# Attention with beacon keys and a gated feed-forward: value products of batches 2 and 3 over 64-row halves

## The chip, the cores and the metric

The kernel runs on one core of one Trainium2 chip. The metric is the device time of one execution in microseconds, lower is better; the time before is the median of three runs. Engines are named as the profile names them: PE is TensorE's matrix products and PEld its weight loads, DVE is VectorE, ACT is ScalarE, POOL is GpSimd and SP is SyncE. The "q" behind an engine's name stands for its queue, in which it also issues transfers (DMAs).

## The reference

There are 8 batches, 8 heads, 576 tokens and a head size of 64. Each batch and head has 16 beacon keys and values, which every query sees; among the tokens themselves the mask is causal. The heads' outputs are put side by side as 512 columns for 4608 tokens and go through a gated feed-forward of width 1536.

```python
k_all = np.concatenate([beacon_k, k], axis=2)
v_all = np.concatenate([beacon_v, v], axis=2)
scores = scale * np.matmul(q, k_all.transpose(0, 1, 3, 2))
scores = np.where(causal, -1000000000.0, scores)
a = np.exp(scores - scores.max(-1, keepdims=True))
a /= a.sum(-1, keepdims=True) + 1e-09
attn = np.matmul(a, v_all)
...
g = x @ w_gate
out = (g * (1.0 / (1.0 + np.exp(-g))) * (x @ w_val)) @ w_out
```

## The kernel before

**Pairs.** Two heads make a pair, so a batch has 4 pairs and the whole has 32. Pair n belongs to batch n // 4: pairs 0 to 3 are batch 0, pairs 8 to 15 are batches 2 and 3. The 592 keys of a head lie in 5 blocks of 128, the last one half filled. The 576 queries lie in 5 blocks (`QBLOCKS`), and query block c needs the key blocks 0 to c, so a head has 1 + 2 + 3 + 4 + 5 = 15 value products (batch 0 does its first two query blocks elsewhere, in `pv_front`).

**What one pair goes through.** Scores for four units A to D (`scores`, TensorE, tile s_ps), the exponential (`exponent`, ScalarE, line 379, tile p), the mask on the diagonal (`mask`, VectorE line 388 or POOL line 392), then the value products (`pv`, TensorE, tile pv_ps), whose stationary side is a block of p, 128 keys by 128 queries, and whose moving side is 64 columns of values and a column of ones that gives the sum. `normalize` (VectorE: the reciprocal at line 493, the product at line 494) writes x. When a batch's four pairs are normalized, `x_transpose` (line 519) makes SP issue five transposes by DMA, x to xT; the gate and value products (`gate_value`, tile gv_ps) read xT, and `project` (tile o_ps) makes the output.

**Two ways of doing the value products.** The constant `WIDE` (line 34) chooses by batch. In batches below `WIDE` the first pass (letter P of the plan) does the 15 products of the pair's first head and the second pass (letter p) those of the second, each over all 128 rows of a key block: line 465. In the other batches every product is cut in two over 64 rows of the key block (rows 0 to 63 and 64 to 127), and each pass has 30 of them. The first pass takes rows 0 to 63 for head 0 and rows 64 to 127 for head 1, in turn; the second pass takes the other half for each. Each head has its own bank of pv_ps. These go through `halves`, whose product stands at line 151, as do all scores, gate, value and output products, which are cut into 64-row halves throughout. When a bank is about to be written from the other row half than before, `halves` first puts in an instruction that waits for the last product into that tile:

```python
if was is not None and was[0] != row:
    last = max((w for (i, _), w in writers.items() if i == at[0]), key=lambda w: w[2])
    if was[3]:
        after(nc.tensor.nop(), last[1], "one bank, two row halves")
```

**What sets the order.** One long string, the plan, written out by hand: each letter emits one piece of work, and every engine takes its instructions in that order. S or s are scores, E an exponential, D or M a mask on VectorE or POOL, P and p the two passes, R a normalization, G and H the two passes of a gate and value unit, F output products, O and o evacuations, V the five transposes x to xT, t one transpose of keys or queries by SP, and l one load issued by POOL. After the first 24, a load waits on POOL for a product two pieces back, so TensorE's progress paces the loads. Four PSUM tiles of two banks each (`take`, `give`) go round among scores, value products, gate units and output.

The letters around the passes of pairs 8 to 15 are

```
8:  Pp          9: PMDtMp      10: PEOlp      11: PEMp
12: PDlRp      13: PlEp        14: PEMDp      15: Pp
```

of which E, M, D, t, O, l and R put nothing on TensorE. After pair 9 pair 10 follows, and after pair 11 pair 12, also with nothing on TensorE between (`oD`, and none). Among the later pairs, over 64-row halves, pair 16 has `PlFFp`, pair 17 `PESFlp`, pair 19 `Pa2Ep` (a and 2 are not on TensorE), and pairs 22 and 23 together `P1Pp2p`.

Of the kernel before, what the change touches and what calls it, by code (L numbers as in the profile page):

```python
# [30 lines left out]
ROWS = S // HALF  # L31


WIDE = 4


FREE_LOADS = 24
# [33 lines left out]
def kernel(  # L71
# [381 lines left out]
    def pv(n, second):  # L453
# [4 lines left out]
        o_ps = pvs[n]  # L458
        if b < WIDE:

# [355 lines left out]
```

## Time and profile before

| | |
|---|---|
| median of 3 runs | 369.63 us (368.88 to 370.25) |
| the profiled execution | 369.36 us, span 367.6 us |
| granted TensorE clock, mean | 0.999 |
| value products over 128 rows (L465) | 456 in pairs 0 to 15, 18.5 to 143.6 us |
| value products over 64 rows (L151) | 960 in pairs 16 to 31, 144.0 to 281.5 us |

The span goes from the first to the last instruction of the profiled execution; the time is that of the whole execution and a little longer. In the profile's first part each engine has its busy time, its share of the span and its count of instructions. The chain that ended last is followed back from the last instruction, at each step to what released it. In a timeline each row is a start in microseconds, a length, the engine, the line, the operation with output and inputs, how many were merged, and in square brackets how long the engine had been idle and what the profile names as the reason. A wait for several semaphores is put down to one of them, which need not be the right one. The slices of the page, 40 equal parts of the span with busy tenths, tell where transfers fill the core's 16 DMA engines:

```profile
PE   7799999989999999999999999999999999999996
...
DMA  8999999999999999999598309301330201100113
```

TensorE's tenths stay at 9 from the tenth slice on; the DMA engines are nearly full up to about the twentieth slice, some 175 us, which takes in pairs 8 to 15.

### The profile page before, as it was taken

How to read it: one execution, taken by the hardware profiler on the slowest of the kernel's cores; microseconds unless marked ns; L12 is line 12 of the kernel's file. 1: busy time of each engine (PE TensorE's matmuls, PEld its weight loads, DVE VectorE, ACT ScalarE, POOL GpSimd, SP SyncE). 2: the span in 40 equal slices, each digit the busy share in tenths (PEclk: the TensorE clock that was granted, in tenths of full speed). 3: DMA queues.
4: the chain of work that ended last, by engine and by line, in shares of the span. 5: the costliest groups of instructions: out<-in, count | busy, mean ns of one | idle time of the engine just before them, and what ended most of it. 6: DMA issues, size and time to landing. Idle time of an engine off the chain costs nothing.

```text
span 367.6 us, 11647 instructions
## 1 busy us (share of the span) xinstructions
PE 355.6 (97%) x5037; PEld 219.9 (60%) x5037; DVE 227.1 (62%) x429; ACT 185.9 (51%) x276; POOL 124.6 (34%) x201
## 2 busy tenths in 40 slices
PE   7799999989999999999999999999999999999996
PEld 3588565655565555555665567556766555555554
DVE  4577786548764676277636683767568735766631
ACT  3874688953576651736774458237913322322201
POOL 8862456972366286770350027000200000000000
PEclk9999999999999999999999999999999999999999
DMA  8999999999999999999598309301330201100113
GB/s 147 162 193 201 204 164 160 147 170 176 158 127 176 175 115 107 112 201 150 63 180 101 86 7 124 67 0 59 68 116 14 54 13 46 60 3 0 60 59 114
DMA packets 143988, 39.88 MB, mean 108 GB/s; under 512 B 130368, under 2 KB 139328, under 8 KB 143936
## 3 DMA queue, kind: packets, MB, share of 16 engines
q0 software_dynamic: 95424, 18.85, 73.0%
q1 hardware_dynamic: 48224, 19.92, 30.1%
q8 instruction: 39, 0.64, 0.7%
q10 hardware_dynamic: 288, 0.36, 0.3%
q14 instruction: 13, 0.11, 0.1%
HBM read 38.27 MB, written 9.44 MB: 130 GB/s over the span
## 4 chain that ended last, share of the span: by engine, by line
PE 88%; DMA 4%; DVE 3%; ACT 2%; issue 1%; POOL 1%; SPq 1%; POOLq 0%; ACTq 0%
PE gv_ps L151 51%; PE o_ps L151 23%; PE s_ps L151 6%; PE pv_ps L151 4%; PE pv_ps L465 4%; DMA xT<-x 2%; DMA qk<-in_q_dram 2%; PE t_ps L283 1%; ACT p L379 1%; DVE x L494 1%; SPq L519 1%; DVE x L427 0%; DVE kT L246 0%; POOL qk L193 0%; DVE p L388 0%
## 5 line engine op out<-in xcount | busy, mean ns | idle before, releaser
L151 PE MATMUL gv_ps<-xT,wg 64*128 64x512 bf16 (+2 forms) x912 | 196.0, 365 | 2.2 <-DVE p L388 1.9
L151 PE MATMUL gv_ps<-xT,wv 64*128 64x512 bf16 (+2 forms) x912 | 197.2, 365 | 0.0
L379 ACT ACTIVATE p<-s_ps 128x832 bf16<-128x832 f32 (+2 forms) x127 | 104.2, 867 | 36.8 <-PE s_ps L151 35.3
L551 ACT ACTIVATE th<-gv_ps 128x512 f32<-128x512 f32 (+2 forms) x114 | 65.5, 574 | 112.1 <-PE gv_ps L151 111.2
L151 PE MATMUL o_ps<-wo,hT 64*128 64x512 bf16 (+2 forms) x912 | 113.9, 365 | 0.2
L556 DVE SCALAR_TENSOR_TENSOR u<-th,gv_ps 128x512 f32<-128x512 f32 (+2 forms) x114 | 74.9, 657 | 59.3 <-ACT th L551 59.0
L151 PEld LDWEIGHTS <-wg 64*128 64x128 bf16 x912 | 83.9, 94 | 41.4 <-issue 1.9
L151 PEld LDWEIGHTS <-wv 64*128 64x128 bf16 x912 | 83.6, 94 | 35.2 <-issue 0.5
L563 DVE SCALAR_TENSOR_TENSOR hT<-gv_ps,u 128x512 bf16<-128x512 f32 (+2 forms) x114 | 75.2, 663 | 3.6
L151 PEld LDWEIGHTS <-hT 64*128 64x128 bf16 x912 | 46.7, 94 | 30.0 <-PE o_ps L151 1.2
L392 POOL TENSOR_SCALAR_AFFINE_SELECT p<-p 128x256 bf16<-128x256 bf16 (+2 forms) x66 | 25.3, 405 | 74.6 <-ACT p L379 72.3
L151 PE MATMUL s_ps<-qT,kT 64*128 64x336 bf16 (+3 forms) x512 | 45.0, 250 | 2.2 <-DVE kT L246 0.5
L202 POOL DMA_DIRECT2D vb<-in_v_dram x40 | 34.0, 854 | 22.7 <-PE gv_ps L151 15.9
L151 PEld LDWEIGHTS <-kT 64*128 64x128 bf16 x512 | 25.2, 94 | 21.9 <-DVE kT L246 1.2
L388 DVE TENSOR_TENSOR p<-p,upper 128x256 bf16<-128x256 bf16 (+2 forms) x77 | 21.4, 298 | 22.3 <-ACT p L379 21.2
L494 DVE TENSOR_TENSOR x<-pv_ps,rec 128x640 bf16<-128x640 f32 (+1 forms) x32 | 25.3, 791 | 1.2
L202 POOL DMA_DIRECT2D qk<-in_q_dram x25 | 21.3, 852 | 11.0 <-PE pv_ps L465 3.5
L246 DVE COPY o_sb<-o_ps 128x512 f32<-128x512 f32 (+2 forms) x22 | 14.0, 663 | 17.8 <-PE o_ps L151 12.8
L202 POOL DMA_DIRECT2D qk<-in_k_dram x25 | 21.1, 844 | 9.3 <-PE s_ps L151 3.9
L493 DVE RECIPROCAL rec<-pv_ps 128x10 f32<-128x10 f32 (+1 forms) x32 | 6.9, 215 | 24.2 <-PE pv_ps L151 16.2
L151 PEld LDWEIGHTS <-p 64*128 64x128 bf16 x960 | 18.4, 94 | 3.4 <-DVE x L494 0.2
L244 ACT ACTIVATE o_sb<-o_ps 128x512 f32<-128x512 f32 (+2 forms) x16 | 8.7, 570 | 22.5 <-PE o_ps L151 21.7
(63 smaller groups left out, 136.6 us busy)
## 6 DMA issues: line engine op xcount, KB each, us to landing
out_dram<-o_sb SPq DMA_DIRECT2D x34, 256.0 KB, 3.4
vb<-in_v_dram POOLq DMA_DIRECT2D x24, 128.0 KB, 7.1
qk<-in_q_dram POOLq DMA_DIRECT2D x20, 128.0 KB, 6.4
qk<-in_k_dram POOLq DMA_DIRECT2D x15, 128.0 KB, 6.8
wv<-in_moe_w_val_dram POOLq DMA_DIRECT2D x4, 384.0 KB, 8.9
wg<-in_moe_w_gate_dram POOLq DMA_DIRECT2D x4, 384.0 KB, 8.7
wo<-in_moe_w_out_dram POOLq DMA_DIRECT2D x2, 768.0 KB, 15.1
qk<-in_k_dram POOLq DMA_DIRECT2D x2, 576.0 KB, 13.4
```

Source lines behind the costliest of these rows:

```text
L151: ins = nc.tensor.matmul(o, lhsT=l, rhs=r, start=start, stop=stop)
L202: return nc.gpsimd.dma_start(dst[p0 : p0 + n, c, :, 0:D], src[b, :, r : r + n, :].rearrange("h j d -> j h d"))
L244: nc.scalar.activation(o, i, ACT.Copy)
L246: eng.tensor_copy(o, i)
L379: nc.scalar.activation(p_of(b, m, u == "A")[:, :, c0 : c0 + w], ps[:, :, 0:w], ACT.Exp, scale=0.125)
L388: nc.vector.tensor_tensor(out=ap, in0=ap, in1=upper[:, None, d : d + w].to_broadcast([P, 2, w]), op=ALU.mult)
L392: nc.gpsimd.affine_select(out=ap, in_=ap, compare_op=ALU.is_ge, fill=0.0, base=d, pattern=[[0, 2], [1, w]], channel_multiplier=-1,)
L465: ins = nc.tensor.matmul(o_ps[:, side, 68 * c : 68 * c + D + 1], lhsT=pt[n % NPT][:, side, col : col + P], rhs=vb[b % 2][:, t, 2 * m + sid ...
L494: nc.vector.tensor_tensor(out=xs[b][:, c0:NKT, P * m : P * m + P].rearrange("p c (h d) -> p h c d", d=D), in0=o[:, :, :, 0:D], in1=rec[:, ...
L551: nc.scalar.activation(th[:, 0:w], gvs[n][:, 0, 0:w], ACT.Tanh, scale=0.5)
L556: nc.vector.scalar_tensor_tensor(out=u[:, 0:w], in0=ths[n][:, 0:w], scalar=1.0, in1=gvs[n][:, 0, 0:w], op0=ALU.add, op1=ALU.mult)
L563: nc.vector.scalar_tensor_tensor(out=hTs[j][:, f, c0:c1], in0=gvs.pop(n)[:, 1, 0 : c1 - c0], scalar=0.5, in1=ths.pop(n)[:, 0 : c1 - c0], o ...
```

## The change

One constant goes from 4 to 2, so that `pv` takes the path over 64-row halves from batch 2 on:

```diff
-WIDE = 4
+WIDE = 2
```

The two paths in `pv`, the first of which batches 2 and 3 leave and the second of which they take:

```python
        if b < WIDE:
            ...
                    ins = nc.tensor.matmul(
                        o_ps[:, side, 68 * c : 68 * c + D + 1],
                        lhsT=pt[n % NPT][:, side, col : col + P],
                        rhs=vb[b % 2][:, t, 2 * m + side, 0 : D + 1],
            ...
                for row in (1, 0) if second else (0, 1):
                    hh = row ^ second
                    r = slice(HALF * row, HALF * row + HALF)
                    halves(
                        ("p", n), hh, row, o_ps[:, hh, 68 * c : 68 * c + D + 1],
                        pt[n % NPT][r, hh, col : col + P], vb[b % 2][r, t, 2 * m + hh, 0 : D + 1],
```

In pairs 8 to 15 a pass thus has 30 weight loads and 30 products over 64 rows, of 128 and 65 columns, where it had 15 and 15 over 128 rows; and `halves` puts its wait between the two passes of each pair. Batches 0 and 1 keep whole rows, batches 4 to 7 keep halves. The plan, the loads and the work of the other engines are as before.

## The prediction

> **What bounds the kernel now.** I read the page first: its opening lines and the chain that ended last.
>
> ```profile
> span 367.6 us, 11647 instructions
> PE 355.6 (97%) x5037; PEld 219.9 (60%) x5037; DVE 227.1 (62%) x429; ACT 185.9 (51%) x276; POOL 124.6 (34%) x201
> PE 88%; DMA 4%; DVE 3%; ACT 2%; issue 1%; POOL 1%; SPq 1%; POOLq 0%; ACTq 0%
> ```
>
> TensorE is busy for 97% of the span and is 88% of the chain. So a microsecond more on TensorE is a microsecond more at the end, unless TensorE would have waited there anyway. Two questions follow: what the eight changed head pairs cost on TensorE, and where TensorE waits behind them. The view of the tile pv_ps has the two forms side by side (nanoseconds min/median/max, first and last start):
>
> ```profile
> L151 PE MATMUL pv_ps<-vb,p x960: 187/189/201, 144.0 to 281.5; 64*128 64x65 bf16 x192
> L465 PE MATMUL pv_ps<-vb,p x456: 190/193/205, 18.5 to 143.6; 128*128 128x65 bf16 x152
> ```
>
> The 189 and 193 ns are latencies of overlapping products and say nothing of the pace. The pace is read from starts, in TensorE's timeline (start, length, operation, count). Pair 13 alone, and pairs 11 and 12 together, over 128 rows:
>
> ```profile
> 110.61 0.34 PE L151 MATMUL s_ps<-qT,kT 64*128 64x240 bf16 x4
> 110.88 1.08 PE L465 MATMUL pv_ps<-vb,p 128*128 128x65 bf16 x30
> 111.90 0.35 PE L151 MATMUL s_ps<-qT,kT 64*128 64x336 bf16 x4
> ```
> ```profile
> 103.38 0.40 PE L151 MATMUL o_ps<-wo,hT 64*128 64x512 bf16 x2
> 103.71 1.99 PE L465 MATMUL pv_ps<-vb,p 128*128 128x65 bf16 x60
> 105.63 0.37 PE L151 MATMUL s_ps<-qT,kT 64*128 64x336 bf16 x4
> ```
>
> The two passes of pair 17, over 64-row halves, apart from each other:
>
> ```profile
> 150.09 0.32 PE L151 MATMUL s_ps<-qT,kT 64*128 64x240 bf16 x4
> 150.25 0.61 PE L151 MATMUL pv_ps<-vb,p 64*128 64x65 bf16 x30
> 150.70 0.34 PE L151 MATMUL s_ps<-qT,kT 64*128 64x336 bf16 x4
> 150.88 0.38 PE L151 MATMUL o_ps<-wo,hT 64*128 64x512 bf16 x2
> 151.09 0.61 PE L151 MATMUL pv_ps<-vb,p 64*128 64x65 bf16 x30
> ```
>
> And pair 19, the one pair over halves whose second pass follows its first with nothing between on TensorE (two windows, the second opening after the first pass ends):
>
> ```profile
> 177.52 0.36 PE L151 MATMUL s_ps<-qT,kT 64*128 64x336 bf16 x4
> 177.70 0.64 PE L151 MATMUL pv_ps<-vb,p 64*128 64x65 bf16 x30
> ```
> ```profile
> 178.40 0.23 PE L151 MATMUL pv_ps<-vb,p 64*128 64x65 bf16 x4
> ```
>
> **The change, part by part.** The built program shows it on TensorE alone: each pair 8 to 15 gets 60 loads and 60 products over 64 rows for 30 and 30 over 128, 240 products more in all; every other queue keeps its order.
>
> *Products.* A pass of 30 half products takes 150.70 - 150.25 = 0.45 us, so two half products, one on each row half, start within 30 ns. A pair over 128 rows takes 111.90 - 110.88 = 1.02, or 34 ns a product with what lies at its edges. Doubling the count therefore costs nothing in pace: 2 x 0.45 = 0.90 against 1.02.
>
> The Trainium skill has a rule that speaks against the change ("TensorE: Matmul & The Clock Gate", section "LDWEIGHTS (loading the stationary operand)"): a weight load takes time by its columns, not by its rows, about 128/1.2 = 107 ns, so a 64-row load is no cheaper than a 128-row one. If loads were served one after another, an estimate from that page is 30 x 107 ns = 3.2 us more for each pair and 26 us in all. The rows of pair 17 deny this: two loads and two products pass in 30 ns, so loads for the two row halves overlap, and I put nothing for them.
>
> *Edges.* From the 240-column scores to the first wide product is 110.88 - 110.61 = 0.27 us; to the first half product it is 150.25 - 150.09 = 0.16. TensorE pays about 0.1 where it passes from half rows to whole rows. The way out is similar: the last wide product of pair 13 starts at 111.77 and the next score at 111.90, 0.13 later, against 0.03 at pair 17. Both go away.
>
> *The new wait.* The second pass writes each bank from the other row half, and `halves` puts a wait on the first pass's last product before it. At pair 19 the second pass starts 178.40 - 177.70 = 0.70 after the first, where a pass takes 0.45: the wait costs 0.25. In all of pairs 8 to 15 the written order has nothing on TensorE between the passes, so all eight pay it. Behind the waiting load stands all of TensorE's queue; ScalarE's exponentials wait for the scores in it, and VectorE's reciprocals for the pair's last product.
>
> *Sum.* A single pair between scores: before 111.90 - 110.61 = 1.29; after 0.16 + 0.70 + 0.45 = 1.31, so +0.02. Bounds 0.00 to +0.05: a pass read at 0.44 to 0.455, before other neighbours. A double, pairs 11 and 12: before 105.63 - 103.38 = 2.25; after 0.21 (151.09 - 150.88) + 2 x (0.70 + 0.45) = 2.51, so +0.26: the edges are saved once, the wait is paid twice. Pairs 9 and 10 between scores: 77.51 - 75.30 = 2.21 before, 0.18 + 2.30 = 2.48 after, +0.27. Pairs 8, 13, 14 and 15 are singles. In all 4 x 0.02 + 0.26 + 0.27 = **+0.61 us** on TensorE (0.5 to 0.75).
>
> **What TensorE waits for behind them.** TensorE's waits from 66 to 146 us, then two rows of its timeline and one of the transfers issued at 70.59:
>
> ```profile
> PE gv_ps L151 <- DVE p L388: 1.9, 2, 1.4
> ```
> ```profile
> 79.24 0.37 PE L151 MATMUL gv_ps<-xT,wg 64*128 64x512 bf16 x1 [1.38 <-DVE p L388]
> ```
> ```profile
> 155.44 0.37 PE L151 MATMUL gv_ps<-xT,wg 64*128 64x512 bf16 x1 [0.19 <-DMA xT<-x]
> ```
> ```profile
> xT<-x SPq DMA_TRANSPOSE x1, 8.5
> ```
>
> The name VectorE in two of them misleads. This gate product needs the transposes into xT of its batch; the last it needs was issued at 70.59 and landed 8.5 later, at 79.11, 0.13 before the product. The stall at 116.96 (idle 0.51) ends alike: issued 109.84, landed 116.71. So TensorE arrives early three times, by 1.38, 0.51 and 0.19 us, and waits for a transfer.
>
> Pairs 8 to 10 (+0.02 and +0.27 = 0.29) lie ahead of the 1.38 us stall, whose transfers began at 66.51, before pair 8 ran: hidden in full; without that cover they cost 0.29.
>
> Pairs 11 to 14 (+0.26, +0.02, +0.02 = 0.30) lie ahead of the 0.51 us stall. But its transposes need pair 11 normalized: VectorE's x ends at 105.90 and SP issues at 105.93. Pair 11's last product would start at 103.38 + 0.21 + 0.70 + 0.44 = 104.73 where it was 104.60, so SP's issue is 0.13 late. If the landing follows, the stall ends 0.13 later; if a backlog of the transfer engines sets it, nothing. SP's next in line, output stores and the transposes for batch 5's scores, also move by 0.13; the scores after pair 14 need transposes that landed by 109.59, 5.3 us early. POOL's paced loads wait for products and move with them. I take **+0.13** (0 to 0.30, the latter without the cover).
>
> Pair 15 (+0.02) ends a little later too: its last product at 142.45 + 0.21 + 0.70 + 0.44 = 143.80 for 143.65, +0.15, and with it the transposes SP issues from 145.00, on which the 155.44 stall ends. TensorE has 0.19 to spare, so the landing decides: +0.13 + 0.15 = **+0.28** if it follows the issue, 0 if not. After 155.44 no TensorE stall above 0.1 us remains that could take it back, so it reaches the end.
>
> The profiled execution took 369.36 us for its span of 367.6; it becomes 369.64. The median of the runs is 369.63, 0.27 above; on it the forecast is 369.63 + 0.28 = **369.9 us**.
>
> **Rivals.** *The cover slides along.* Landings move with the products and all 0.61 stays: 369.63 + 0.61 = 370.2. For it: loads are paced by TensorE's progress. Against: the first stall's transfers start before pair 8.
>
> *Late transposes, the slower side.* Issued 0.13 to 0.28 later, the transposes for batches 2 and 3 fall behind one more of POOL's loads and land one place later. Places are 1.48 us apart (77.63 and 79.11). Two slips: 0.28 + 2 x 1.48 = 3.24, 372.9; it counts as slower only from the second slip, since one gives 371.4. For it: the transposes into xT take from 3.0 to 8.1 us to land in these two groups. Against: the delay is small beside POOL's 0.85 us for issuing one load.
>
> *The wait is hidden.* Then a single gains 1.29 - (0.16 + 0.90) = 0.23 and a double 2.25 - (0.21 + 1.80) = 0.24; six groups give 1.4, so 368.2. For it: pairs 22 and 23, with passes interleaved, run 120 products in 1.82 us without a gap. Against: the order here is pass, pass of the same pair, eight times, as in pair 19.
>
> *It does not do what it says*: the built order excludes that.
>
> **How the numbers follow.** Half a per cent, 1.85 us, is about what a measurement tells from no change. Forecast 0.60; cover slides 0.17; late transposes 0.15, of which 0.12 beyond the half per cent; wait hidden 0.08, of which 0.04 beyond. So faster 0.04, same 0.84, slower 0.12. The forecast's own range is 0 to +0.61 on a median that moves with runs between 368.88 and 370.25: 369.0 to 370.8. To leave out no more than 2 in 10 it reaches almost to one slip, 371.3.
>
> **What would show it.** Pairs 8 to 15 run 60 products each, the second pass starting 0.70 after the first; a single stands 1.31 between scores, a double 2.5. The stall at 79.24 ends where it did, with about 1.1 us idle for 1.38; those at 116.96 and 155.44 end 0.1 to 0.3 later. A wait much above 0.25, edges that stay at 0.1, or landings moved by over a microsecond would make it wrong.

## The result, and the profile after

The changed kernel takes 375.64 us (median of 4 runs, 374.27 to 376.06) where the kernel before takes 369.62 (4 runs, 368.88 to 370.25): a ratio of 1.0136 (95% interval 1.0094 to 1.0178), slower by about 6 us. Measured again, seven times, it took 373.59 for 370.0: 1.0084 (1.0056 to 1.0113). So the change costs 0.8 to 1.4%, where 369.0 to 371.3 us had been forecast.

The page of the changed kernel, its first lines, the row of TensorE's instruction transfers and the chain that ended last, and then the row of the transfers in the kernel before (packets, megabytes, share of the engines' time):

```profile
span 374.3 us, 12127 instructions
PE 358.7 (96%) x5277; PEld 216.0 (58%) x5277; DVE 227.8 (61%) x429; ACT 186.0 (50%) x276; POOL 124.7 (33%) x201
...
q8 instruction: 41, 0.67, 0.8%
...
PE 86%; DMA 6%; ACT 3%; DVE 1%; issue 1%; SPq 1%; POOL 1%; POOLq 0%; ACTq 0%
```
```profile
q8 instruction: 39, 0.64, 0.7%
```

The span grew by 6.7 us and TensorE's busy time by 3.1, so TensorE also stands idle more. The 240 loads and 240 products more are there (5277 for 5037). The q8 row, which I had passed over in the page of before, is the one that mattered: a packet of 16 KB for every 256 instructions of TensorE.

What was predicted for the pairs themselves came out. TensorE's timeline after, pairs 11 and 12 together and pair 13 alone:

```profile
105.82 0.40 PE L151 MATMUL o_ps<-wo,hT 64*128 64x512 bf16 x2
106.04 2.47 PE L151 MATMUL pv_ps<-vb,p 64*128 64x65 bf16 x120
108.34 0.36 PE L151 MATMUL s_ps<-qT,kT 64*128 64x336 bf16 x4
...
113.31 0.34 PE L151 MATMUL s_ps<-qT,kT 64*128 64x240 bf16 x4
113.47 1.31 PE L151 MATMUL pv_ps<-vb,p 64*128 64x65 bf16 x60
114.62 0.34 PE L151 MATMUL s_ps<-qT,kT 64*128 64x336 bf16 x4
```

The double takes 108.34 - 105.82 = 2.52 us (predicted 2.51) and the single 114.62 - 113.31 = 1.31 (predicted 1.31). Pair 14 took 0.14 more than pair 13. The time went elsewhere. TensorE's waits after, from 66 to 150 us, and the places in its timeline:

```profile
PE gv_ps L151 <- DMA xT<-x: 2.0, 1, 2.0
PE gv_ps L151 <- issue: 1.9, 1, 1.9
PE pv_ps L151 <- issue: 0.5, 1, 0.5
```
```profile
76.42 0.53 PE L151 MATMUL pv_ps<-vb,p 64*128 64x65 bf16 x23
77.45 2.11 PE L151 MATMUL pv_ps<-vb,p 64*128 64x65 bf16 x97 [0.50 <-issue]
...
79.58 0.38 PE L151 MATMUL gv_ps<-xT,wg 64*128 64x512 bf16 x1
...
82.18 0.38 PE L151 MATMUL gv_ps<-xT,wv 64*128 64x512 bf16 x1
84.48 0.37 PE L151 MATMUL gv_ps<-xT,wg 64*128 64x512 bf16 x1 [1.93 <-issue]
...
121.33 0.47 PE L151 MATMUL gv_ps<-xT,wg 64*128 64x512 bf16 x1 [1.98 <-DMA xT<-x]
...
162.09 0.37 PE L151 MATMUL gv_ps<-xT,wg 64*128 64x512 bf16 x1 [0.76 <-DMA xT<-x]
```

Two of the waits are of a kind that the trace of before does not show at these places: TensorE stops in the middle of a run of equal products (after the 23rd half product of pair 9; within the gate and value products of one unit), with no semaphore to wait for. "issue" is the profile's word for idle time that nothing explains. Counted in the built program, the first instruction behind each pause is number 2498 and number 2754 of TensorE's stream: 256 apart. The records of queue q8 have one packet of 16,384 bytes (256 instructions of 64 bytes) at 74.61 to 75.91 us and the next at 82.11 to 82.99; each time TensorE went on 1.5 us after the packet's end (77.45, 84.48). The stall at 79.24 that was to hide pairs 8 to 10 is gone, as what TensorE was late there by, pair 9's pause included, has used it up.

Behind the second pause the changed kernel is 2.4 us behind the one before at the same work (95 us), 2.9 at the transposes of batch 2, and 6.1 after them. There SP issues the fourth transpose, the one needed, at 113.34 for 109.84: 2.6 late from the start, and 0.9 because the first issue took 2.08 us for 1.23. It took 2.13 us itself for 1.28, and landed at 121.08 for 116.71. The stall is 1.98 for 0.51, and a stretch at half the clock follows, in the table by windows (start and end, length, busy time and count of PE, PEld, DVE, ACT and POOL, granted clock, transfer share, GB/s):

```profile
115.00:121.30 6.30, 4.28 (x98) 2.47 (x95) 3.57 (x9) 3.99 (x5) 4.27 (x10) 1.00 1.68 149
121.30:125.00 3.70, 3.67 (x22) 1.74 (x24) 0.00 (x0) 0.00 (x0) 0.00 (x0) 0.54 2.11 187
125.00:135.00 10.00, 10.00 (x103) 5.45 (x99) 6.49 (x11) 5.94 (x9) 2.73 (x5) 1.00 1.52 136
```

At a clock of 0.54 the 3.7 us cost about (1 - 0.54) x 3.7 = 1.7. Another such stretch lies at 12.3 to 15.7 us, ahead of every changed pair (0.9 us by 68 us). The kernel before has mean clocks of 0.991 to 0.995 in some of its runs, as one or two such stretches would give, so that part of this execution's 6 us need not be the change's.

### The profile page after: what moved, and what is told of

Read it like the earlier page. It is cut to its first block, busy times and chain, and to the rows that moved or that the text cites. A ratio compares the mean times of both kernels' runs of the same rounds, so it can differ in the third digit from the quotient of the medians.

```text
span 374.3 us, 12127 instructions
## 1 busy us (share of the span) xinstructions
PE 358.7 (96%) x5277; PEld 216.0 (58%) x5277; DVE 227.8 (61%) x429; ACT 186.0 (50%) x276; POOL 124.7 (33%) x201
## 4 chain that ended last, share of the span: by engine, by line
PE 86%; DMA 6%; ACT 3%; DVE 1%; issue 1%; SPq 1%; POOL 1%; POOLq 0%; ACTq 0%
PE gv_ps L151 51%; PE o_ps L151 21%; PE pv_ps L151 5%; PE s_ps L151 5%; DMA xT<-x 4%; PE pv_ps L465 2%; DMA qk<-in_q_dram 2%; ACT p L379 1%; SPq L519 1%; PE t_ps L283 1%; DVE x L494 0%; ACT th L551 0%; POOL qk L193 0%; ACT qT L244 0%; PE s_ps L166 0%
## 5 line engine op out<-in xcount | busy, mean ns | idle before, releaser
L151 PE MATMUL gv_ps<-xT,wg 64*128 64x512 bf16 (+2 forms) x912 | 198.2, 367 | 4.8 <-DMA xT<-x 2.7
L151 PEld LDWEIGHTS <-hT 64*128 64x128 bf16 x912 | 45.0, 94 | 31.7 <-PE o_ps L151 1.2
L202 POOL DMA_DIRECT2D vb<-in_v_dram x40 | 34.0, 853 | 23.8 <-PE gv_ps L151 15.7
L151 PEld LDWEIGHTS <-p 64*128 64x128 bf16 x1440 | 26.9, 94 | 6.2 <-PE pv_ps L151 1.7
L151 PE MATMUL pv_ps<-vb,p 64*128 64x65 bf16 x1440 | 29.4, 190 | 1.1 <-issue 0.5
## 6 DMA issues: line engine op xcount, KB each, us to landing
wo<-in_moe_w_out_dram POOLq DMA_DIRECT2D x2, 768.0 KB, 14.5
```

What stands on the lines that cost most here:

```text
L151: ins = nc.tensor.matmul(o, lhsT=l, rhs=r, start=start, stop=stop)
L202: return nc.gpsimd.dma_start(dst[p0 : p0 + n, c, :, 0:D], src[b, :, r : r + n, :].rearrange("h j d -> j h d"))
```

## The experiments

**Theory.** TensorE's instructions come from memory in pieces of 256. The packet for the next piece is asked for about when TensorE enters the present one. While transfers fill the DMA engines it starts later: 3.5 and 4.1 us after that at the two borders around pair 9 in the kernel before, 4.1 and 4.7 in the changed kernel, though 0.9 to 2.7 at the next ones in the kernel before. It takes about 1 us or a little more, and TensorE can go on 1.5 us after it: near 7 us in all around pair 9. A piece that is used up sooner makes TensorE wait. Half products are used up twice as fast as whole ones, 60 instructions in 0.45 us. In the kernel before, the pieces around pair 9 lasted 7.2 and 14.5 us (entered at 70.04, 77.21 and 91.75); after, the second would have lasted 5.1 without its pause. **Rivals:** the waits for the row half, or the half products themselves in one of the pairs, delay TensorE and then the transfers.

The first test moves the borders of the pieces by more instructions in the warm-up, small products on unused data ahead of all stages, with the pairs as they are in the changed kernel (a load and a product each: 184 instructions more here, 48 in the kernel after it).

```diff
-    warm(11, TOK)
-    warm(6, P)
+    warm(8, TOK)
+    warm(101, 32)
```

> The changed kernel with 184 more TensorE instructions in the warm-up (92 small products more), pairs 8 to 15 untouched; so the borders of the 256-instruction pieces in which TensorE's instructions arrive fall elsewhere in pairs 9 and 10. Fetch theory (a piece is asked for when the one before it begins and takes about 7 us in this phase): the pause of 2.1 us at 82 us goes, the one inside pair 9 stays below 1 us, no half-rate clock near 120 us; time 369.5 to 371.5. Rival (the wait between the passes makes normalization and transposes late): borders do not matter, 375 to 376.

Measured: 373.12 us for 370.5, 1.0082 (1.0048 to 1.0115). The pause near 82 us is gone, one of 0.29 us stands in pair 9, and the large one has moved to a border behind pair 14, in the timeline:

```profile
117.13 0.32 PE L151 MATMUL s_ps<-qT,kT 64*128 64x240 bf16 x4
119.18 0.39 PE L151 MATMUL o_ps<-wo,hT 64*128 64x512 bf16 x2 [1.73 <-issue]
```

So the pauses go with the borders, but the time was missed: the piece with pairs 13 and 14 had not been seen to be too short. The second of these kernels has 48 more:

```diff
-    warm(11, TOK)
-    warm(6, P)
+    warm(10, TOK)
+    warm(31, 32)
```

> The changed kernel with 48 more TensorE instructions in the warm-up, so that one 256-instruction piece holds nearly all of pairs 9 and 10, and another nearly all of pairs 11 and 12. Fetch theory: TensorE runs through such a piece in about 4 us and waits some 3 us for the next, a pause of 2 to 4 us near 79 us and of 1 to 3 us near 107 us; time 376 to 381. Rival (wait between the passes, late transposes): as the changed kernel, 375 to 376.

Measured: 373.38, 1.009 (1.0054 to 1.0125), below what was expected by either. One pause, of the size expected, some us behind the place named:

```profile
80.26 0.39 PE L151 MATMUL gv_ps<-xT,wv 64*128 64x512 bf16 x1
83.03 0.58 PE L151 MATMUL gv_ps<-xT,wg 64*128 64x512 bf16 x1 [2.39 <-issue]
```

The one expected near 107 us did not come. The control is the kernel before with the first of these warm-ups.

> The kernel before with the same longer warm-up as the first of these runs, a control. Fetch theory: the pieces last at least 7 us where transfers are dense, so no pause; 369 to 370.5. Any theory in which the warm-up itself costs: more than 371.

Measured: 374.16, 1.0098 (1.006 to 1.0136): missed, and the most useful miss. Without any change to the pairs the kernel before loses 3.7 us, partly by a pause in its later half products; two longer stalls for transposes into xT stand ahead of it:

```profile
119.56 0.37 PE L151 MATMUL gv_ps<-xT,wg 64*128 64x512 bf16 x1 [1.83 <-DMA xT<-x]
...
159.91 0.37 PE L151 MATMUL gv_ps<-xT,wg 64*128 64x512 bf16 x1 [2.05 <-DMA xT<-x]
...
232.52 1.51 PE L151 MATMUL pv_ps<-vb,p 64*128 64x65 bf16 x87
235.29 0.23 PE L151 MATMUL pv_ps<-vb,p 64*128 64x65 bf16 x3 [1.26 <-issue]
```

In this execution, 6.0 us behind the kernel before at its end, the pause makes 1.5, the two stalls (1.83 us for 0.51 and 2.05 for 0.19) 3.2, and the rest lies ahead of them. No pause precedes those stalls, so the theory does not explain them, and their cause stays open. On top of this warm-up the change costs nothing (373.12 for 374.16). Instructions that do no work of the kernel can thus cost as much as the change did when measured again; that the borders are the reason is shown for the pauses alone.

The next kernels put halves into some pairs alone; the first also ran beside the two above.

```diff
-WIDE = 2
+HALVES = (9, 10)
...
-        if b < WIDE:
+        if b < 4 and n not in HALVES:
```

> 64-row halves in pairs 9 and 10 alone, the other six pairs of batches 2 and 3 over 128 rows. Fetch theory: without pair 8's 60 extra instructions the border of the pieces falls near the middle of pairs 9 and 10, the piece before it lasts some 6.2 us and the one after 8.8; a pause of at most 1 us, hidden by the wait for xT at 79 us: 369 to 371. Rival (each pair adds its share, by its wait or by lateness): a quarter to a half of the 6 us, 371.2 to 373.

Measured: 371.0, 1.0006 (0.9974 to 1.0039). TensorE's waits from 66 to 150 us are this one line, with no "issue":

```profile
PE gv_ps L151 <- DVE rec L493: 0.2, 1, 0.2
```

The closest border was passed with some 0.2 us to spare, counted by the 1.5 us from packet to product. One pause of 0.13 us stands at 232. Next, pair 8 besides (`HALVES = (8, 9, 10)`):

> 64-row halves in pairs 8, 9 and 10, the others of batches 2 and 3 over 128 rows: to the run with pairs 9 and 10 alone, pair 8 is added, whose own price on TensorE is 0.02 us. Fetch theory: pair 8's 60 extra instructions move the borders of the 256-instruction pieces to where they stood in the changed kernel, so both pauses come back, about 0.5 us inside pair 9 and about 2 us near 82 us; 371.5 to 374.5, at least 1 us above the run with pairs 9 and 10 alone. Rival (each pair adds its own share): at most 0.3 us above it, 370.5 to 371.3.

Measured: 374.53, 1.0099 (1.007 to 1.0129). The two pauses stand at instructions 2498 and 2754, as expected, and a third one, which I had not expected, in the later pairs that no part of the change touches. The second and the third are:

```profile
81.98 0.38 PE L151 MATMUL gv_ps<-xT,wv 64*128 64x512 bf16 x1
83.91 0.37 PE L151 MATMUL gv_ps<-xT,wg 64*128 64x512 bf16 x1 [1.56 <-issue]
...
229.80 1.54 PE L151 MATMUL pv_ps<-vb,p 64*128 64x65 bf16 x89
233.93 0.23 PE L151 MATMUL pv_ps<-vb,p 64*128 64x65 bf16 x1 [2.58 <-issue]
```

Behind the second pause this kernel is 1.9 us behind the one before; the third, with 3.4 us at half the clock, adds 4.4. Pair 8's 60 instructions cost nothing in pair 8 itself: behind it, at 75 us, this kernel is 0.04 us later than the one before. The other single pairs with halves, `HALVES = (8, 13, 14, 15)`:

> 64-row halves in pairs 8, 13, 14 and 15 alone; pairs 9 to 12, which follow each other two by two, over 128 rows. Fetch theory: no 256-instruction piece is run through in less than its fetch takes, no pause at a border; 369.5 to 371.2. Rival (each of the eight pairs adds its share of the 6 us): 372 to 374.

Measured: 369.53, 0.9984 (0.9964 to 1.0003), no pause: eight passes of halves and four of the waits, with no loss. TensorE's waits from 66 to 150 us are one line:

```profile
PE gv_ps L151 <- DVE x L494: 1.4, 1, 1.4
```

Then the wait between the passes. In this kernel the plan interleaves the passes of pairs 9 with 10 and 11 with 12, so that other halves fill the wait, with as many instructions as in the changed kernel (parts of two lines of the plan):

```diff
-'PMDtMpoDPEOlpRlSG'
+'PMDtMoDPEOlppRlSG'
...
-'EDSFPEMpPDlRpSFEFRVS'
+'EDSFPEMPDlpRpSFEFRVS'
```

> The changed kernel with the passes of pairs 9 and 10, and of 11 and 12, interleaved (first, first, second, second), so that the wait between the passes is hidden for four of the eight pairs: 1.0 us less of waiting on TensorE. Fetch theory: TensorE comes to the border of its piece earlier and waits there as much longer, the pauses near 77 and 82 us end where they ended; 374 to 376.5, not more than 1 us below the changed kernel. Rival (the wait between the passes is what costs): 370 to 372.5.

Measured: 372.0, 1.0046 (1.0023 to 1.0069), below what the theory expects and inside the range of the rival. The kernel as changed, measured beside it:

> The changed kernel itself beside these on the same chip. Both theories: 374 to 376; fetch theory: pauses without a semaphore at the same two instructions, 256 apart, near 77 and 82 us in this execution too, whatever the time at which it reaches them.

Measured: 373.59, as said above and a little below what was expected. Of the two pauses only that at 2754 came; TensorE passed number 2498 at 76.22, 1.3 us after its packet's end, without one. The large pause of the interleaved kernel and its pairs 11 and 12, and then the pause of the changed one:

```profile
82.56 0.38 PE L151 MATMUL gv_ps<-xT,wv 64*128 64x512 bf16 x1
84.24 0.37 PE L151 MATMUL gv_ps<-xT,wg 64*128 64x512 bf16 x1 [1.30 <-issue]
...
105.58 0.40 PE L151 MATMUL o_ps<-wo,hT 64*128 64x512 bf16 x2
105.79 1.99 PE L151 MATMUL pv_ps<-vb,p 64*128 64x65 bf16 x120
107.61 0.37 PE L151 MATMUL s_ps<-qT,kT 64*128 64x336 bf16 x4
```
```profile
81.19 0.38 PE L151 MATMUL gv_ps<-xT,wv 64*128 64x512 bf16 x1
83.37 0.37 PE L151 MATMUL gv_ps<-xT,wg 64*128 64x512 bf16 x1 [1.81 <-issue]
```

Interleaved, the double takes 107.61 - 105.58 = 2.03 us for 2.52, less than over whole rows (2.25). So the wait is a real term, half a microsecond in a double. The new order gave 1.6 us in all (the two intervals just overlap), where the theory allowed 1, and the pause at instruction 2754 stays. The traces side with the theory: counted from where each kernel stood ahead of pair 8, both are 1.2 us later than the kernel before when that pause ends, and at the end the interleaved one has gained 0.9.

The last two settle it. Halves in pairs 9 and 10 alone had cost nothing. Now the warm-up gets 60 instructions more, as many as pair 8's halves add, and pair 8 stays as it was; beside it the kernel before with the same warm-up.

```diff
-    warm(11, TOK)
+    warm(10, TOK)
     warm(6, P)
+    warm(31, 32)
```

> Halves in pairs 9 and 10 alone, pair 8 over 128 rows, and the warm-up of 11 large and 6 medium products made of 10 large, 6 medium and 31 narrow ones, so that TensorE has 60 instructions more ahead of the stages and no other change. That puts the borders of its 256-instruction pieces where pair 8's halves put them in the kernel with halves in pairs 8 to 10. Instruction-fetch theory: the same kernel without the 60 took 371.0 with no pause; now one of 1 to 2 us near 82 us comes back and perhaps one near 231 us, in the middle of a pass, with no semaphore before it; 372.5 to 375. Rival (pair 8's own halves, not the position, made that kernel slower): no pause near 82 us and 370.5 to 371.5.

Measured: 373.87 for 369.36, 1.0096 (1.0062 to 1.013), as the theory expects. Both pauses came back, the first shorter than the 1 to 2 us expected, the second, which had been put down as possible, larger:

```profile
83.86 0.38 PE L151 MATMUL gv_ps<-xT,wv 64*128 64x512 bf16 x1
84.83 0.37 PE L151 MATMUL gv_ps<-xT,wg 64*128 64x512 bf16 x1 [0.59 <-issue]
...
231.23 1.53 PE L151 MATMUL pv_ps<-vb,p 64*128 64x65 bf16 x89
235.06 0.20 PE L151 MATMUL pv_ps<-vb,p 64*128 64x65 bf16 x1 [2.29 <-issue]
```

The late pause stands behind the 89th half product of the same run as with pair 8 in halves. The piece that it ends was entered at 229.97 and used up in 2.6 us, as pairs 22 and 23 run interleaved in it. Both programs have the same number of instructions on TensorE. The kernel before with the 184 has four more, and there it stands behind the 87th: four instructions are two loads and two products. A position counted in instructions, to the very one, is what neither a semaphore nor a slow transfer of data would give. In this execution the two places with a pause make 3.4 of the 5.8 us by which it ends behind the kernel before; 2.0 lie ahead of pair 8, where a stretch at half the clock stands at 11.8 us.

> The kernel before with the same warm-up of 60 instructions more and nothing else. Instruction-fetch theory: the pieces that hold pairs 8 to 12 last 7.7 and 12.2 us there, about the 7 us that a fetch takes in this phase or more, so no pause between 60 and 150 us; late pieces last 4.1 us or more; 369 to 371.5. Rival (the longer warm-up by itself costs, whatever the pieces): slower than 372 without a pause in TensorE's stream.

Measured: 368.99, 0.9983 (0.9957 to 1.0009), no pause; TensorE's waits from 66 to 150 us are this line:

```profile
PE gv_ps L151 <- DVE p L388: 1.8, 2, 1.3
```

So 60 instructions more cost nothing by themselves.

All kernels, by the difference of the median from that of the kernel before measured beside it; the pauses are idle times before a product, "issue", from 60 to 300 us of the profiled execution:

| kernel | pauses, us | median, us | before, us | difference |
|---|---|---|---|---|
| halves in 8, 13, 14, 15 | none | 369.53 | 370.0 | -0.5 |
| before, 60 more ahead | none | 368.99 | 369.36 | -0.4 |
| halves in 9, 10 | 0.13 | 371.0 | 370.5 | +0.5 |
| change, interleaved | 0.14, 1.30 | 372.0 | 370.0 | +2.0 |
| change, 184 more | 0.29, 1.73, 0.27 | 373.12 | 370.5 | +2.6 |
| change, 48 more | 2.39 | 373.38 | 370.5 | +2.9 |
| change, second time | 1.81 | 373.59 | 370.0 | +3.6 |
| before, 184 more | 1.26 | 374.16 | 370.5 | +3.7 |
| halves in 9, 10, 60 more | 0.59, 2.29 | 373.87 | 369.36 | +4.5 |
| halves in 8, 9, 10 | 0.68, 1.56, 2.58 | 374.53 | 370.0 | +4.5 |
| the change | 0.50, 1.93 | 375.64 | 369.62 | +6.0 |

The kernels without a pause of more than 0.13 us lie within 0.5 us of the kernel before, and all others are slower by 2 us or more. Counted in the built programs, every one of the 16 pauses stands before an instruction whose number leaves 194 when divided by 256, as 2498 and 2754 do; none of TensorE's other waits does. The pauses alone do not make up all of a difference (1.26 us for 3.7 in the kernel before with 184 more). None of these versions is clear of the kernel before on the faster side.

## Why the prediction was wrong

**The step that failed** is the one on products: "Doubling the count therefore costs nothing in pace", with which the supply of twice as many instructions was put at nothing. It holds for the engine, where the pass of 30 halves still takes 0.45 us, and fails for the supply. 480 instructions more are two pieces more (41 packets for 39), and the pieces around pairs 8 to 10 now run out before the next has come. I had priced loads, products, edges and waits on TensorE and looked for what is late among semaphores and data transfers; the transfer of the instructions was in the page and got no price. From the trace of before it could be had: there the packet for instruction 2498 landed at 75.01, so at 1.5 us from packet to product TensorE could have gone on at 76.51, and it came at 77.21. The 0.7 us to spare is less than the 0.95 that halves in pairs 8 and 9 take off the same piece (7.17 us, and 6.22 without its pause); halves in pair 9 without those in pair 8 take 0.5, and there no pause came. For number 2754 the packet landed at 82.27, so TensorE could have gone on at 83.8; it came at 91.75. In the changed kernel, with the 180 instructions more of pairs 8 to 10, it stood there at 82.5.

**Right.** The wait of 0.25 us and the saved edges: single 1.31, double 2.52. Pairs 9 and 10 took 79.40 - 76.23 = 3.17 us between scores; at the pause two products start 0.69 apart (76.76 and 77.45) that would else follow each other in 0.02, so 2.50 without it, for 2.48 predicted.

**The first cover.** The stall of 1.38 us at 79.24 was to hide 0.29. It hid that, and the first pause too: at 81.5 us the changed kernel was 0.3 us behind, having been 0.9 behind at 68. The second pause lies behind the stall, at 82.18, where nothing covers it.

**The transposes.** They were to land 0.13 and 0.28 us later. They landed 4.4 late (121.08 for 116.71), of which 2.6 came in from ahead and nearly all the rest from SP's two longer issues, and, for batch 3, 6.6 late (161.95 for 155.31), of which 6.1 came in from ahead. The prediction's own test, "landings moved by over a microsecond", was met. The rival "late transposes" had a right place, but not a delay of 0.13 us that makes one slip another place: most of the delay is brought in from ahead, the two pauses among it. Whether loads of POOL stood in the way of the slow issues was not tested.

**The sizes.** In the second profiled execution of the changed kernel, whose clock is 1.000, it stands 0.7 us ahead of the kernel before at 81.5 us, 1.3 behind at 95, 1.8 at 116, 2.7 at 125 and 2.35 at the end: 2.0 for the second pause, 0.4 up to 116 for pairs 11 to 14, 0.9 for the stall of batch 2, and 0.4 of it won back. That is the smallest of its seven times (371.68); what the longer ones add was not profiled there.

**Open.** Why SP's issue of a transpose takes 2.1 us at times instead of 1.25, and how much of that the shifted schedule causes; the kernel before with 60 more, which has no pause and loses nothing, has issues of 2.25 and 2.14 us in these two groups too. Why the kernel before with 184 more waits longer for its transposes with no pause ahead. How far the fetch of 7 us depends on which transfers run beside it: only its place was moved here, not the load on the DMA engines. How often the half clock comes with and without the change: the four runs first measured have 0.990 to 0.994, of seven later ones one has 0.994 and the others 0.999 or 1.000.

## What to carry to other kernels

Count the instructions, not only their time: an edit that doubles the count of short instructions on one engine shortens the time that a piece of its program lasts, and where the transfers are dense the next piece may not be there in time. In a trace, look for idle time with no releaser in the middle of equal work, count the instructions between two such places, and compare with the packets of the instruction queue. When a small edit gives a strange loss, add the same number of harmless instructions ahead in the kernel before: here that alone made -0.4 us (60) or +3.7 us (184, of which the profile puts only a part down to a border).

## What the runs showed of the hardware

- TensorE's program comes in packets of 16,384 bytes, 256 instructions. Past 240 us, where the DMA engines are little used, the packet of the next piece started from 2.3 us before to 1.4 us after TensorE's first product of the present one; around 70 to 90 us it started 2.3 to 5.2 us after it, and 3.8 to 4.8 where a pause followed. TensorE went on 1.25 to 1.55 us after the packet's end wherever it had paused. The Trainium skill ("Runtime: NRT & Kernel Launch", section "Instruction fetch mechanics") has the same 256-instruction blocks, and says that crossing into the next is mostly hidden, since instructions are dispatched more slowly than they are fetched. The runs differ: crossing cost 0.1 to 2.6 us at the borders listed above, where half products are used up at 60 instructions in 0.45 us.
- With an idle time of 1.98 us (up to 121.33) 3.4 us at half the clock set in, and so with 2.58 us (up to 233.93, with halves in pairs 8 to 10); with 2.39 us (up to 83.03, the change with 48 more) it was 6.8. With 1.93 us (up to 84.48), 2.05 (up to 159.91, the kernel before with 184 more) and 2.29 (up to 235.06, with halves in 9 and 10 and 60 more) the clock stayed full.
- Products of one row half, interleaved between two pairs, run 120 in 1.82 us from the first to what follows (105.79 to 107.61), where the same 120 took 2.30 with the two waits (106.04 to 108.34).
